# Linear attention and a gated ffn on one core: norm with tokens on partitions, weight conversion on three engines, and two first layers ahead of their second layers

## The chip, the cores and the metric

The kernel runs on one core of a Trainium2 chip. The metric is the device time of one execution in microseconds (us), the median of several executions on the same chip.

## The reference

The input of the ffn is the output of a linear attention whose result is normalized by its root mean square. Cut to what matters:

```python
# q, k, v: (8 batches, 8 heads, 576 tokens, 64) float32
kv  = np.einsum('bhsd,bhse->bhde', k, v)
out = np.einsum('bhsd,bhde->bhse', q, kv)
rms = np.sqrt(np.mean(out * out, axis=-1, keepdims=True) + 1e-06)
attn_out = (out / rms * g_norm).astype(np.float32)

x = attn_out.transpose(0, 2, 1, 3).reshape(4608, 512)
# w_gate, w_val: (512, 1536), w_out: (1536, 512), all float64
gate = 1.0 / (1.0 + np.exp(-(x @ w_gate)))
val  = x @ w_val
return (gate * val @ w_out).astype(np.float32)
```

The weights are float64, so the kernel gets each value as two 32-bit words, and it makes float32 of them for TensorE. There are 36 blocks of 128 x 512 weights: 12 each of w_gate, w_val and w_out.

## The kernel before

The 4608 tokens are cut into 9 chunks of 512. A chunk has 12 steps of first layer (one for each 128 columns of w_gate and w_val) and 4 steps of second layer. The attention of the next batch is cut into 16 small steps (kv, q, u and x for each of four pairs of heads), and one is put in front of each step of a chunk. A kv step makes k^T v of a pair of heads, a q step transposes q, a u step multiplies the two, and an x step makes the ffn's input of the result. The product of gate and value that a step of first layer leaves for the second is called gv. The attention of batch 0 runs alone at the start.

The conversion of a block is seven instructions on VectorE and an add on GpSimd:

```python
        vec.tensor_scalar(out=xf, in0=hi.bitcast(FP32), scalar1=HI_MAX, scalar2=-HI_MAX, op0=ALU.min, op1=ALU.max)
        vec.tensor_scalar(out=y, in0=x, scalar1=0x7FFFFFFF, scalar2=None, op0=ALU.bitwise_and)
        vec.scalar_tensor_tensor(out=yf, in0=yf, scalar=HI_MIN, in1=xf, op0=ALU.is_ge, op1=ALU.mult)
        # y: sign, exponent and the upper 20 bits of the fraction, as a float32.
        vec.tensor_scalar(out=x, in0=y, scalar1=0x07FFFFFF, scalar2=3, op0=ALU.bitwise_and, op1=ALU.logical_shift_left)
        vec.scalar_tensor_tensor(out=y, in0=y, scalar=0xC0000000, in1=x, op0=ALU.bitwise_and, op1=ALU.bitwise_or)
        # x: the lower 32 bits of the fraction, scaled by the power of two that sign and exponent are.
        vec.tensor_scalar(out=x, in0=y, scalar1=0xFF800000, scalar2=None, op0=ALU.bitwise_and)
        vec.scalar_tensor_tensor(out=xf, in0=lo, scalar=2.0 ** -52, in1=xf, op0=ALU.mult, op1=ALU.mult)
        ...
        nc.gpsimd.tensor_tensor(out=flat, in0=xf, in1=yf, op=ALU.add)
```

The norm has channels on partitions. The sum over a head's 64 channels is therefore a matmul with a matrix of ones, whose result is repeated on all channels, and root and reciprocal run over 128 x 576 values:

```python
        def u_step(m):
            ...
                nc.tensor.matmul(ps[:, i, 0:HS], kvs[m % 3], qT[m][:, HS * i:HS * i + HS], start=True, stop=True)
            nc.scalar.copy(out=uT[m]..., in_=ps[:, :, 0:HS])
            nc.vector.tensor_tensor(out=sq[m], in0=uT[m], in1=uT[m], op=ALU.mult)

        def x_step(m):
            ...
                nc.tensor.matmul(ps[:, i, 0:HS], ones, sq[m][:, HS * i:HS * i + HS], start=True, stop=True)
            nc.scalar.activation(out=rs..., in_=ps[:, :, 0:HS], func=AF.Sqrt, bias=eps, scale=1.0)
            nc.vector.reciprocal(rs, rs)
            ...   # xT = uT * g_col * rs on VectorE
```

The order of the steps converts w_gate and w_val one step ahead of their use in chunk 0, and then all of w_out at once:

```python
    for c in range(NG):
        ahead = attention(c + 1) if c + 1 < B else []
        for i, step in enumerate(ffn(c)):        # 12 steps of first layer, 4 of second
            if ahead:
                ahead.pop(0)()
            while done < min(2 * i + 4, 2 * NFT) or i >= NFT - 1 and done < len(units):
                convert(done)
                done += 1
            step()
```

## Time and profile before

| | before |
|---|---|
| time | 1356.22 us, 1355.11 to 1356.49 in 4 runs |
| span of the profiled execution | 1354.3 us |
| attention of batch 0, before the first conversion | 53.4 us |
| from there to the end of chunk 0's first layer | 134.3 us |
| from there to chunk 1's first matmul | 90.7 us |
| the rest | 1075.9 us |

The profile is read here from the stretches that are not full. In the slices of the page each digit is a tenth of busy time of one fortieth of the span; where TensorE has no idle time, as in the first full chunk of this kernel (busy for 137.65 of 137.65 us at a granted clock of 1.00), nothing is to be had but less work for TensorE. In this kernel its row shows 9 from the eighth slice on, and the whole question is what fills the first seven. In the lines PE is TensorE, PEld its weight loads, DVE VectorE, ACT ScalarE, POOL GpSimd, and SP SyncE; the granted clock is the share of TensorE's full clock that the chip allowed. In the lines of a timeline the columns are start, duration, engine, line, operation, result and operands with their shapes, and in brackets the idle time before and what ended it. The lines themselves stand in the prediction.

### The profile page before, as it was taken

The page shows a single profiled execution, that of the slowest core. Times are in us where ns is not written, and L with a number is a line of the kernel's source. Part 1 is how long each engine was busy: PE and PEld are TensorE (multiplying, and loading weights), DVE is VectorE, ACT ScalarE, POOL GpSimd, SP SyncE. Part 2 cuts the span into 40 slices and gives each one's busy share as a digit, 9 for nine tenths or more (in the row PEclk, how much of TensorE's full clock was granted, in tenths as well). Part 3 has the DMA queues.
Part 4 walks back from the last instruction along what each step waited for, and adds up shares of the span by engine and source line. Part 5 has one row for each costly group of instructions (what it writes and reads, how often), then busy time and mean ns, then how long its engine had stood idle before and what let it go on. Part 6 is the DMA issues. An engine that isn't in the chain of part 4 may idle for free.

```text
span 1354.3 us, 9279 instructions
## 1 busy us (share of the span) xinstructions
PE 1260.2 (93%) x3808; PEld 589.2 (44%) x3808; DVE 456.6 (34%) x623; ACT 169.3 (13%) x239; POOL 72.6 (5%) x78
## 2 busy tenths in 40 slices
PE   4578764999999999999999999999999999999998
PEld 3233321444444444444444444444444444444443
DVE  3899999421322223222321332132212221100100
ACT  1100100111211121112111111111112110000000
POOL 0143333000000000000000000000000000000000
PEclk9699885899999999999999999999999999999999
DMA  9244332011101110211020101110100000000000
GB/s 221 57 125 136 106 109 93 24 52 35 27 24 52 35 27 15 60 30 33 16 60 27 32 19 50 36 27 25 42 1 0 15 16 0 0 23 8 0 1 31
DMA packets 61770, 57.23 MB, mean 42 GB/s; under 512 B 40224, under 2 KB 52512, under 8 KB 61728
## 3 DMA queue, kind: packets, MB, share of 16 engines
q1 hardware_dynamic: 51200, 28.32, 8.5%
q0 software_dynamic: 5184, 18.88, 4.4%
q10 hardware_dynamic: 5344, 9.44, 2.0%
q8 instruction: 30, 0.49, 0.2%
q14 instruction: 12, 0.10, 0.0%
HBM read 47.19 MB, written 9.44 MB: 42 GB/s over the span
## 4 chain that ended last, share of the span: by engine, by line
PE 83%; DVE 13%; issue 2%; DMA 1%; ACT 0%; SPq 0%; POOL 0%; POOLq 0%; DVEq 0%; ACTq 0%
PE mm L226 49%; PE mm L235 27%; DVE cy L110 3%; PE at L186 2%; PE at L195 2%; DVE cy L114 2%; DVE cy L111 2%; PE at L165 2%; DVE rs L199 1%; DVE cx L109 1%; DVE cx L113 1%; DVE cx L116 1%; PE at L176 1%; DMA v<-in_v_dram 1%; DVE gv L230 1%
## 5 line engine op out<-in xcount | busy, mean ns | idle before, releaser
L226 PE MATMUL mm<-xT,wg 128*128 128x512 f32 x864 | 399.7, 606 | 27.1 <-POOL wg L120 27.1
L235 PE MATMUL mm<-wo,gv 128*128 128x512 f32 x864 | 389.2, 606 | 32.2 <-POOL wo L120 32.2
L226 PE MATMUL mm<-xT,wv 128*128 128x512 f32 x864 | 389.3, 593 | 8.7 <-POOL wv L120 8.7
L230 DVE TENSOR_TENSOR gv<-mm,sg 128x512 f32<-128x512 f32 x108 | 74.6, 691 | 597.6 <-PE mm L226 597.5
L235 PEld LDWEIGHTS mm<-wo,gv 128*128 128x128 f32 x864 | 165.5, 193 | 240.1 <-issue 188.0
L226 PEld LDWEIGHTS mm<-xT,wv 128*128 128x128 f32 x864 | 163.4, 190 | 218.7 <-issue 202.3
L226 PEld LDWEIGHTS mm<-xT,wg 128*128 128x128 f32 x864 | 161.9, 193 | 204.6 <-issue 170.1
L199 DVE RECIPROCAL rs<-rs 128x576 f32<-128x576 f32 x32 | 120.0, 3752 | 134.4 <-ACT rs L197 134.4
L228 ACT ACTIVATE sg<-mm 128x512 f32<-128x512 f32 x108 | 64.5, 597 | 610.2 <-PE mm L226 610.2
L237 ACT COPY out<-mm 128x512 f32<-128x512 f32 x36 | 21.1, 585 | 397.1 <-PE mm L235 397.1
L190 DVE TENSOR_TENSOR sq<-uT 128x576 f32<-128x576 f32 x32 | 26.0, 811 | 62.4 <-ACT uT L189 62.4
L195 PE MATMUL at<-sq,ones 128*128 128x288 f32 x128 | 38.9, 428 | 5.1 <-DVE sq L190 5.1
L165 PEld LDWEIGHTS at<-v,k 96*64 96x64 f32 x768 | 27.4, 148 | 29.3 <-issue 27.3
L179 DVE COPY qT<-at 128x288 f32<-128x288 f32 x64 | 37.5, 665 | 7.4 <-PE at L176 7.3
L186 PE MATMUL at<-qT,kv 128*128 128x288 f32 x128 | 39.6, 435 | 0.4 <-DVE qT L179 0.4
L165 PE MATMUL at<-v,k 96*64 96x64 f32 x768 | 31.9, 237 | 7.1 <-DMA v<-in_v_dram 6.6
L110 DVE TENSOR_SCALAR cy<-cx 128x512 uint32<-128x512 uint32 x36 | 38.0, 1054 | 1.2
L195 PEld LDWEIGHTS at<-sq,ones 128*128 128x128 f32 x128 | 25.2, 201 | 23.0 <-issue 13.4
L189 ACT COPY uT<-at 128x576 f32<-128x576 f32 x32 | 20.4, 639 | 117.4 <-PE at L186 106.4
L186 PEld LDWEIGHTS at<-qT,kv 128*128 128x128 f32 x128 | 25.9, 205 | 18.9 <-issue 12.7
L176 PEld LDWEIGHTS at<-ident,q 96*128 96x128 f32 x192 | 21.3, 151 | 26.0 <-issue 22.0
L176 PE MATMUL at<-ident,q 96*128 96x96 f32 x192 | 23.2, 261 | 9.9 <-DMA q<-in_q_dram 6.5
(28 smaller groups left out, 305.5 us busy)
## 6 DMA issues: line engine op xcount, KB each, us to landing
k<-in_k_dram SPq DMA_DIRECT2D x32, 288.0 KB, 3.4
v<-in_v_dram SPq DMA_DIRECT2D x32, 288.0 KB, 3.9
q<-in_q_dram SPq DMA_DIRECT2D x64, 144.0 KB, 3.0
out_dram<-out ACTq DMA_DIRECT2D x36, 256.0 KB, 2.0
st<-in_moe_w_gate_dram POOLq DMA_DIRECT2D x12, 512.0 KB, 4.1
st<-in_moe_w_val_dram POOLq DMA_DIRECT2D x12, 512.0 KB, 4.3
st<-in_moe_w_out_dram POOLq DMA_DIRECT2D x12, 512.0 KB, 3.6
g_col<-in_g_norm_dram ACTq DMA_DIRECT2D x2, 0.2 KB, 4.4
```

What stands on the lines that cost most here:

```text
L110: vec.tensor_scalar(out=y, in0=x, scalar1=0x7FFFFFFF, scalar2=None, op0=ALU.bitwise_and)
L111: vec.scalar_tensor_tensor(out=yf, in0=yf, scalar=HI_MIN, in1=xf, op0=ALU.is_ge, op1=ALU.mult)
L165: nc.tensor.matmul(ps[HD * e:HD * e + HD, 0, 0:HD], kin[:, e, js], vin[:, e, js], start=(j == 0), stop=(j == NJ - 1))
L176: nc.tensor.transpose(ps[:, j // 3, c0:c0 + NP], qin[:, j].rearrange("p e d -> p (e d)"), ident[0:NP, 0:NP])
L179: nc.vector.tensor_copy(out=qT[m].rearrange("q (p i t) -> q i t p", i=2, t=3)[:, i], in_=ps[:, i, 0:HS].rearrange("q (t p) -> q t p", t=3))
L186: nc.tensor.matmul(ps[:, i, 0:HS], kvs[m % 3], qT[m][:, HS * i:HS * i + HS], start=True, stop=True)
L195: nc.tensor.matmul(ps[:, i, 0:HS], ones, sq[m][:, HS * i:HS * i + HS], start=True, stop=True)
L199: nc.vector.reciprocal(rs, rs)
L226: nc.tensor.matmul(ps, w[name, f][:, m, :], xT[c][:, m, :], start=(m == 0), stop=(m == NMT - 1))
L228: nc.scalar.activation(out=sg, in_=pg, func=AF.Sigmoid)
L230: nc.vector.tensor_tensor(out=gv[f], in0=pv, in1=sg, op=ALU.mult)
L235: nc.tensor.matmul(ps, gv[f][:, P * t:P * t + P], w["wo", f], start=(f == 0), stop=(f == NFT - 1))
```

## The change

The intent is to shorten the first seven slices in three ways.

1. **Norm.** The u step computes its result with tokens on partitions (six matmuls, with q transposed as the weights). A head's 64 channels then lie side by side in a row, so the mean of squares is one reduce, and the root and the reciprocal are over 96 x 12 values in place of 128 x 576. The x step is six transposes back, and ScalarE copies the result out with the gain as its scale. The tokens stay in the permuted order of the loads, and the stores put the rows back.
2. **Conversion.** The absolute value goes to ScalarE, the limiting to GpSimd, five instructions stay on VectorE, the add stays on GpSimd.
3. **Order.** The first layers of chunks 0 and 1 both precede their second layers, so w_out is converted one block per step of chunk 1's first layer.

The core of the diff:

```diff
+    def limit(u):
+        x = sb.tile([P, UW], U32, tag="cx", name="cx", bufs=1)
+        a = sb.tile([P, UW], FP32, tag="ca", name="ca", bufs=1)
+        nc.gpsimd.tensor_scalar(out=x.bitcast(FP32), in0=hi.bitcast(FP32), scalar1=HI_MAX, scalar2=-HI_MAX,
+                                op0=ALU.min, op1=ALU.max)
+        nc.scalar.activation(out=a, in_=hi.bitcast(FP32), func=AF.Abs)
+        ranged[u] = x, a
...
-        vec.tensor_scalar(out=xf, in0=hi.bitcast(FP32), scalar1=HI_MAX, scalar2=-HI_MAX, op0=ALU.min, op1=ALU.max)
-        vec.tensor_scalar(out=y, in0=x, scalar1=0x7FFFFFFF, scalar2=None, op0=ALU.bitwise_and)
-        vec.scalar_tensor_tensor(out=yf, in0=yf, scalar=HI_MIN, in1=xf, op0=ALU.is_ge, op1=ALU.mult)
+        vec.scalar_tensor_tensor(out=yf, in0=a, scalar=HI_MIN, in1=xf, op0=ALU.is_ge, op1=ALU.mult)
...      (four more instructions on VectorE as before, with a buffer z of their own)
+        limit(u + 1)
...
         def u_step(m):
+            for j in range(NJ):
+                nc.tensor.matmul(ps[0:NP, j // JH, c0:c0 + P], qT[m][:, j // JH, NP * (j % JH):NP * (j % JH) + NP],
+                                 kvs[m % 2], start=True, stop=True)
+            nc.scalar.activation(out=sq, in_=u, func=AF.Square)
+            nc.vector.tensor_reduce(out=ms..., in_=sq..., axis=AX.X, op=ALU.add)
+            nc.scalar.activation(out=ms, in_=ms, func=AF.Sqrt, bias=eps[0:NP], scale=1.0 / HD)
+            nc.vector.reciprocal(ms, ms)
+            nc.vector.tensor_tensor(out=xn[m]..., in0=u..., in1=ms.unsqueeze(3).to_broadcast(...), op=ALU.mult)
         def x_step(m):
+            for j in range(NJ):
+                nc.tensor.transpose(ps[:, j // JH, c0:c0 + NP], xn[m][...], ident[0:NP, 0:NP])
+                nc.scalar.activation(out=chunk(c)[:, m, o:o + n], in_=ps[:, i, r:r + n], func=AF.Copy, scale=g_col)
...
+    todo = [(0, s) for s in ffn_in(0)] + [(1, s) for s in ffn_in(1)] + [(1, s) for s in ffn_out(0) + ffn_out(1)]
+    for c in range(2, NG):
+        todo += [(c, s) for s in ffn_in(c) + ffn_out(c)]
+    for i, (c, step) in enumerate(todo):
+        if c != last:
+            for a in ahead:      # what is left of the attention of the batch before
+                a()
+            ahead = attention(fed) if fed < B and fed <= c + 1 else []
...
+        while done < min(2 * i + 4, 2 * NFT) or i >= NFT and done < min(NFT + i + 2, len(units)):
```

The change also copies q transposed on ScalarE instead of VectorE, loads two pairs of heads ahead instead of three, puts a pair's x step before the next pair's u step, and issues the stores of the result on SyncE's queue instead of ScalarE's.

More of the change, by code (lines that the diff above doesn't have):

```diff
@@ L14 @@
 ALU = mybir.AluOpType
+AX = mybir.AxisListType
 HI_MIN = struct.unpack("<f", struct.pack("<I", 0x38100000))[0]
@@ L42 @@
     NP = S // NJ
-    HS = S // 2
     NMT = DM // P
@@ L47 @@
     NG = T // G
-    NLD = 3
+    NLD = 2
     NST = 3
@@ L72, in load_pair @@
         pairs[n].append(t)
-    for n in range(NLD):
-        load_pair(n)
     units = []
@@ L85 @@
     assert UW == DM
-    staged, w = {}, {}
+    staged, ranged, w = {}, {}, {}
     def load_unit(u):
@@ L93, in load_unit, with words @@
         nc.gpsimd.dma_start(out=staged[u], in_=src)
+    def words(u):
+        t = staged[u]
+        if len(units[u][3]) == 3:
+            t = t.rearrange("p m f -> p (m f)")
+        t = t.bitcast(U32).rearrange("p (n two) -> p n two", two=2)
+        return t[:, :, 0], t[:, :, 1]
+    def limit(u):
+        if u >= len(units):
+            return
+        lo, hi = words(u)
+        x = sb.tile([P, UW], U32, tag="cx", name="cx", bufs=1)
[4 more added lines that the diff above has]
+        ranged[u] = x, a
@@ L95, in convert @@
     def convert(u):
         name, f, src, shape = units[u]
-        if len(shape) == 3:
-            words = staged[u].rearrange("p m f -> p (m f)").bitcast(U32)
-        else:
-            words = staged[u].bitcast(U32)
-        words = words.rearrange("p (n two) -> p n two", two=2)
-        lo, hi = words[:, :, 0], words[:, :, 1]
-        x = sb.tile([P, UW], U32, tag="cx", name="cx")
+        lo, hi = words(u)
+        x, a = ranged.pop(u)
         y = sb.tile([P, UW], U32, tag="cy", name="cy")
-        xf, yf = x.bitcast(FP32), y.bitcast(FP32)
+        z = sb.tile([P, UW], U32, tag="cz", name="cz")
@@ L106, in convert @@
+        xf, yf, zf = x.bitcast(FP32), y.bitcast(FP32), z.bitcast(FP32)
         vec = nc.vector
-        vec.tensor_scalar(out=xf, in0=hi.bitcast(FP32), scalar1=HI_MAX, scalar2=-HI_MAX, op0=ALU.min, op1=ALU.max)
-        vec.tensor_scalar(out=y, in0=x, scalar1=0x7FFFFFFF, scalar2=None, op0=ALU.bitwise_and)
-        vec.scalar_tensor_tensor(out=yf, in0=yf, scalar=HI_MIN, in1=xf, op0=ALU.is_ge, op1=ALU.mult)
-        vec.tensor_scalar(out=x, in0=y, scalar1=0x07FFFFFF, scalar2=3, op0=ALU.bitwise_and, op1=ALU.logical_shift_left)
@@ L114, in convert @@
-        vec.scalar_tensor_tensor(out=y, in0=y, scalar=0xC0000000, in1=x, op0=ALU.bitwise_and, op1=ALU.bitwise_or)
-        vec.tensor_scalar(out=x, in0=y, scalar1=0xFF800000, scalar2=None, op0=ALU.bitwise_and)
-        vec.scalar_tensor_tensor(out=xf, in0=lo, scalar=2.0 ** -52, in1=xf, op0=ALU.mult, op1=ALU.mult)
+        vec.scalar_tensor_tensor(out=yf, in0=a, scalar=HI_MIN, in1=xf, op0=ALU.is_ge, op1=ALU.mult)
+        vec.tensor_scalar(out=z, in0=y, scalar1=0x07FFFFFF, scalar2=3, op0=ALU.bitwise_and, op1=ALU.logical_shift_left)
@@ L118, in convert @@
+        vec.scalar_tensor_tensor(out=y, in0=y, scalar=0xC0000000, in1=z, op0=ALU.bitwise_and, op1=ALU.bitwise_or)
+        vec.tensor_scalar(out=z, in0=y, scalar1=0xFF800000, scalar2=None, op0=ALU.bitwise_and)
+        vec.scalar_tensor_tensor(out=zf, in0=lo, scalar=2.0 ** -52, in1=zf, op0=ALU.mult, op1=ALU.mult)
+        limit(u + 1)
         t = const.tile(shape, FP32, name=f"{name}{f}")
         flat = t.rearrange("p m f -> p (m f)") if len(shape) == 3 else t
-        nc.gpsimd.tensor_tensor(out=flat, in0=xf, in1=yf, op=ALU.add)
+        nc.gpsimd.tensor_tensor(out=flat, in0=zf, in1=yf, op=ALU.add)
@@ L121, in convert @@
         w[name, f] = t
         load_unit(u + NST)
+    load_pair(0)
     for u in range(NST):
         load_unit(u)
+    for n in range(1, NLD):
+        load_pair(n)
     ident = const.tile([P, P], FP32, name="ident")
-    ones = const.tile([P, P], FP32, name="ones")
     eps = const.tile([P, 1], FP32, name="eps")
     g_col = const.tile([P, 1], FP32, name="g_col")
-    kvs = [const.tile([P, P], FP32, name=f"kv{i}") for i in range(3)]
+    kvs = [const.tile([P, P], FP32, name=f"kv{i}") for i in range(2)]
@@ L137 @@
     nc.vector.memset(eps, 1e-6)
-    nc.vector.memset(ones, 0.0)
-    for e in range(2):
-        nc.vector.memset(ones[HD * e:HD * e + HD, HD * e:HD * e + HD], 1.0 / HD)
     for kv in kvs:
@@ L153, in at_ps @@
         return psum.tile([P, 2, 512], FP32, tag="at", name="at")
+    JH = NJ // 2
     def attention(b):
-        qT, uT, sq = {}, {}, {}
+        qT, xn = {}, {}
         def kv_step(m):
             kin, vin, _ = pairs[NHP * b + m]
-            kv = kvs[m % 3]
+            kv = kvs[m % 2]
             ps = at_ps()
@@ L174, in q_step @@
             for j in range(NJ):
-                c0 = NP * (j % 3)
-                nc.tensor.transpose(ps[:, j // 3, c0:c0 + NP], qin[:, j].rearrange("p e d -> p (e d)"), ident[0:NP, 0:NP])
-            qT[m] = sb.tile([P, S], FP32, tag="qT", name="qT")
-            for i in range(2):
-                nc.vector.tensor_copy(out=qT[m].rearrange("q (p i t) -> q i t p", i=2, t=3)[:, i],
-                                      in_=ps[:, i, 0:HS].rearrange("q (t p) -> q t p", t=3))
+                c0 = NP * (j % JH)
+                nc.tensor.transpose(ps[:, j // JH, c0:c0 + NP], qin[:, j].rearrange("p e d -> p (e d)"), ident[0:NP, 0:NP])
+            qT[m] = sb.tile([P, 2, JH * NP], FP32, tag="qT", name="qT")
+            nc.scalar.copy(out=qT[m], in_=ps[:, :, 0:JH * NP])
             load_pair(NHP * b + m + NLD)
@@ L184, in u_step @@
             ps = at_ps()
-            for i in range(2):
-                nc.tensor.matmul(ps[:, i, 0:HS], kvs[m % 3], qT[m][:, HS * i:HS * i + HS], start=True, stop=True)
-            uT[m] = sb.tile([P, S], FP32, tag="uT", name="uT")
-            sq[m] = sb.tile([P, S], FP32, tag="sq", name="sq")
-            nc.scalar.copy(out=uT[m].rearrange("q (i s) -> q i s", i=2), in_=ps[:, :, 0:HS])
-            nc.vector.tensor_tensor(out=sq[m], in0=uT[m], in1=uT[m], op=ALU.mult)
+            for j in range(NJ):
+                c0 = P * (j % JH)
+                nc.tensor.matmul(ps[0:NP, j // JH, c0:c0 + P], qT[m][:, j // JH, NP * (j % JH):NP * (j % JH) + NP],
+                                 kvs[m % 2], start=True, stop=True)
+            u = ps[0:NP, :, 0:JH * P]
+            sq = sb.tile([NP, 2, JH * P], FP32, tag="sq", name="sq", bufs=1)
+            ms = sb.tile([NP, 2, 2 * JH], FP32, tag="ms", name="ms")
+            xn[m] = sb.tile([NP, 2, JH * P], FP32, tag="xn", name="xn", bufs=1)
+            nc.scalar.activation(out=sq, in_=u, func=AF.Square)
+            nc.vector.tensor_reduce(out=ms.rearrange("p i n -> p (i n)"),
+                                    in_=sq.rearrange("p i (n d) -> p (i n) d", d=HD), axis=AX.X, op=ALU.add)
+            nc.scalar.activation(out=ms, in_=ms, func=AF.Sqrt, bias=eps[0:NP], scale=1.0 / HD)
+            nc.vector.reciprocal(ms, ms)
+            nc.vector.tensor_tensor(out=xn[m].rearrange("p i (n d) -> p i n d", d=HD),
+                                    in0=u.rearrange("p i (n d) -> p i n d", d=HD),
+                                    in1=ms.unsqueeze(3).to_broadcast([NP, 2, 2 * JH, HD]), op=ALU.mult)
         def x_step(m):
             ps = at_ps()
-            for i in range(2):
-                nc.tensor.matmul(ps[:, i, 0:HS], ones, sq[m][:, HS * i:HS * i + HS], start=True, stop=True)
-            rs = sb.tile([P, S], FP32, tag="rs", name="rs", bufs=1)
-            nc.scalar.activation(out=rs.rearrange("q (i s) -> q i s", i=2), in_=ps[:, :, 0:HS],
-                                 func=AF.Sqrt, bias=eps, scale=1.0)
-            nc.vector.reciprocal(rs, rs)
+            for j in range(NJ):
+                c0 = NP * (j % JH)
+                nc.tensor.transpose(ps[:, j // JH, c0:c0 + NP], xn[m][:, j // JH, P * (j % JH):P * (j % JH) + P],
+                                    ident[0:NP, 0:NP])
             s0 = 0
@@ L202, in x_step @@
                 c, o = divmod(S * b + s0, G)
-                n = min(G - o, S - s0)
-                nc.vector.scalar_tensor_tensor(out=chunk(c)[:, m, o:o + n], in0=uT[m][:, s0:s0 + n], scalar=g_col,
-                                               in1=rs[:, s0:s0 + n], op0=ALU.mult, op1=ALU.mult)
+                i, r = divmod(s0, S // 2)
+                n = min(G - o, S // 2 - r)
+                nc.scalar.activation(out=chunk(c)[:, m, o:o + n], in_=ps[:, i, r:r + n], func=AF.Copy, scale=g_col)
                 s0 += n
@@ L209, in attention @@
         for t in range(NHP + 2):
-            for step, m in ((kv_step, t), (u_step, t - 1), (q_step, t), (x_step, t - 2)):
+            for step, m in ((kv_step, t), (x_step, t - 2), (q_step, t), (u_step, t - 1)):
                 if 0 <= m < NHP:
@@ L213, in attention @@
         return steps
+    gv = {}
     def mm_ps():
         return psum.tile([P, 512], FP32, tag="mm", name="mm", bufs=4)
-    def ffn(c):
-        gv = {}
-        def in_step(f):
-            pg, pv = mm_ps(), mm_ps()
-            for ps, name in ((pg, "wg"), (pv, "wv")):
-                for m in range(NMT):
-                    nc.tensor.matmul(ps, w[name, f][:, m, :], xT[c][:, m, :], start=(m == 0), stop=(m == NMT - 1))
-            sg = sb.tile([P, G], FP32, tag="sg", name="sg")
-            nc.scalar.activation(out=sg, in_=pg, func=AF.Sigmoid)
-            gv[f] = sb.tile([P, G], FP32, tag="gv", name="gv", bufs=NFT + 1)
-            nc.vector.tensor_tensor(out=gv[f], in0=pv, in1=sg, op=ALU.mult)
-        def out_step(t):
-            ps = mm_ps()
-            for f in range(NFT):
-                nc.tensor.matmul(ps, gv[f][:, P * t:P * t + P], w["wo", f], start=(f == 0), stop=(f == NFT - 1))
-            ot = sb.tile([P, DM], FP32, tag="out", name="out")
-            nc.scalar.copy(out=ot, in_=ps)
-            nc.scalar.dma_start(out=out[G * c + P * t:G * c + P * t + P, :], in_=ot)
-        return [lambda f=f: in_step(f) for f in range(NFT)] + [lambda t=t: out_step(t) for t in range(G // P)]
@@ new lines, in in_step @@
+    def in_step(c, f):
+        pg, pv = mm_ps(), mm_ps()
+        for ps, name in ((pg, "wg"), (pv, "wv")):
+            for m in range(NMT):
+                nc.tensor.matmul(ps, w[name, f][:, m, :], xT[c][:, m, :], start=(m == 0), stop=(m == NMT - 1))
+        sg = sb.tile([P, G], FP32, tag="sg", name="sg")
+        nc.scalar.activation(out=sg, in_=pg, func=AF.Sigmoid)
+        gv[c, f] = sb.tile([P, G], FP32, tag="gv", name="gv", bufs=2 * NFT)
+        nc.vector.tensor_tensor(out=gv[c, f], in0=pv, in1=sg, op=ALU.mult)
@@ new lines, in store, with out_step @@
+    def store(c, t, ot):
+        r0 = 0
+        while r0 < P:
+            b, s = divmod(G * c + P * t + r0, S)
+            j, p = divmod(s, NP)
+            n = min(P - r0, NP - p)
+            dst = out[S * b:S * b + S, :].rearrange("(p j) d -> j p d", j=NJ)[j, p:p + n, :]
+            nc.sync.dma_start(out=dst, in_=ot[r0:r0 + n])
+            r0 += n
+    def out_step(c, t):
+        ps = mm_ps()
+        for f in range(NFT):
+            nc.tensor.matmul(ps, gv[c, f][:, P * t:P * t + P], w["wo", f], start=(f == 0), stop=(f == NFT - 1))
+        ot = sb.tile([P, DM], FP32, tag="out", name="out")
+        nc.scalar.copy(out=ot, in_=ps)
+        store(c, t, ot)
@@ L242, with ffn_in, ffn_out @@
+    def ffn_in(c):
+        return [lambda f=f: in_step(c, f) for f in range(NFT)]
+    def ffn_out(c):
+        return [lambda t=t: out_step(c, t) for t in range(G // P)]
+    limit(0)
     for step in attention(0):
@@ L246 @@
     done = 2
-    for c in range(NG):
-        ahead = attention(c + 1) if c + 1 < B else []
-        for i, step in enumerate(ffn(c)):
-            if ahead:
-                ahead.pop(0)()
-            while done < min(2 * i + 4, 2 * NFT) or i >= NFT - 1 and done < len(units):
-                convert(done)
-                done += 1
-            step()
-        assert not ahead
+    ahead = []
+    fed = 1
+    todo = [(0, s) for s in ffn_in(0)] + [(1, s) for s in ffn_in(1)] + [(1, s) for s in ffn_out(0) + ffn_out(1)]
+    for c in range(2, NG):
+        todo += [(c, s) for s in ffn_in(c) + ffn_out(c)]
+    last = -1
+    for i, (c, step) in enumerate(todo):
[3 more added lines that the diff above has]
+            ahead = attention(fed) if fed < B and fed <= c + 1 else []
+            fed += bool(ahead)
+            last = c
+        if ahead:
+            ahead.pop(0)()
+        while done < min(2 * i + 4, 2 * NFT) or i >= NFT and done < min(NFT + i + 2, len(units)):
+            convert(done)
+            done += 1
+        step()
+    assert fed == B and not ahead
 _INS = ['q', 'k', 'v', 'g_norm', 'moe_w_gate', 'moe_w_val', 'moe_w_out']
```

## The prediction

> **What bounds the kernel now.** I read the page's first two parts, then the busy time of each engine by stretch, then the timeline of VectorE and GpSimd inside the stretches that are not full.
>
> The page says that TensorE is the bound on average, and the slices say where it is not: the first eight of forty.
>
> ```profile
> PE 1260.2 (93%) x3808; PEld 589.2 (44%) x3808; DVE 456.6 (34%) x623; ACT 169.3 (13%) x239; POOL 72.6 (5%) x78
> ...
> PE   4578764999999999999999999999999999999998
> ...
> DVE  3899999421322223222321332132212221100100
> ```
>
> The stretches were cut at events of the timeline: 53.37 us is the first instruction of the weight conversion, 187.70 the end of the first layer of chunk 0, 278.39 the first matmul of chunk 1. The fourth row is one whole chunk with a batch of attention in it, the last a whole chunk without. Columns: length, busy us and instructions of each engine, granted clock, DMA share, GB/s.
>
> ```profile
> 0.00:53.37 53.37, 24.58 (x176) 18.31 (x176) 28.76 (x40) 9.27 (x11) 3.11 (x9) 0.87 0.69 157
> 53.37:187.70 134.33, 104.05 (x308) 45.98 (x308) 128.82 (x211) 14.41 (x20) 49.96 (x50) 0.92 0.38 116
> 187.70:278.39 90.69, 59.36 (x133) 23.31 (x133) 64.94 (x87) 4.46 (x7) 19.50 (x21) 0.70 0.19 61
> 278.39:416.04 137.65, 137.65 (x441) 65.50 (x441) 36.27 (x44) 20.15 (x28) 0.00 (x0) 1.00 0.12 34
> 1103.42:1227.02 123.60, 123.60 (x289) 54.72 (x289) 8.29 (x12) 10.79 (x17) 0.00 (x0) 1.00 0.02 9
> ```
>
> From 278.39 us on TensorE never stops: a chunk is 288 matmul instructions at 123.60/288 = 0.429 us (82.4 us of first layer, 41.2 of second), and a batch of attention costs it 137.65 - 123.60 = 14.05 us. Before that, 53.37 us is a chain of attention for batch 0, in the next 134 us VectorE is 96% busy (conversion is the bound), and in the next 91 us TensorE waits for the converted w_out. The waits of that third stretch (who waited for whom: us, times, longest) say so:
>
> ```profile
> PEld mm L235 <- POOL wo L120: 49.2, 12, 4.5
> ...
> PE mm L235 <- POOL wo L120: 32.2, 12, 3.7
> ```
>
> One conversion of a block, from the timeline of VectorE and GpSimd (start, duration):
>
> ```profile
> 205.73 1.36 POOL L120 TENSOR_TENSOR wo<-cx,cy 128x512 f32<-128x512 f32 x1 [2.97 <-DVE cx L117]
> 206.01 1.37 DVE L110 TENSOR_SCALAR cy<-cx 128x512 uint32<-128x512 uint32 x1
> 207.41 0.69 DVE L111 SCALAR_TENSOR_TENSOR cy<-cy,cx 128x512 f32<-128x512 f32 x1
> 208.13 0.43 DVE L113 TENSOR_SCALAR cx<-cy 128x512 uint32<-128x512 uint32 x1
> 208.60 0.69 DVE L114 SCALAR_TENSOR_TENSOR cy<-cy,cx 128x512 uint32<-128x512 uint32 x1
> 209.32 0.43 DVE L116 TENSOR_SCALAR cx<-cy 128x512 uint32<-128x512 uint32 x1
> 209.78 0.69 DVE L117 SCALAR_TENSOR_TENSOR cx<-st,cx 128x512 f32<-128x512 uint32 x1
> 210.39 0.42 DVE L109 TENSOR_SCALAR cx<-st 128x512 f32<-128x512 f32 x1
> 210.57 1.36 POOL L120 TENSOR_TENSOR wo<-cx,cy 128x512 f32<-128x512 f32 x1 [2.97 <-DVE cx L117]
> ```
>
> The period is 210.57 - 205.73 = 4.84 us. L110 takes 1.37 us where L113, of the same kind, takes 0.43: it stands still for 0.94 us while GpSimd adds. Without that a block is 3.90 us.
>
> [...]the squaring at 93.99 us (two SBUF inputs) took 1.32 us beside a GpSimd add against 0.76 alone. [...]gv takes 691.
>
> **The change, part by part.**
>
> *Second layers after both first layers.* w_out's 12 blocks now convert one per step of chunk 1's first layer. A step is 6.87 us of TensorE plus about 0.9 of attention; VectorE needs about 4.9 for the block and 0.69 for gv. They hide, and chunk 0's second layer later runs at the full rate, 41.2 us.
>
> *Norm with tokens on partitions.* On VectorE a pair of heads now costs a reduce of 768[...], a reciprocal of 12 (3752/576 x 12, under 0.2), a multiply of 768[...] and the kv copies 0.45: 2.5 us. It was 3.75 + 0.81 + 1.33 + 1.03 (xT) + 0.45 = 7.4. In the steady chunks VectorE had time anyway, so this is worth nothing there. On TensorE, differences between step starts in the steady chunk give kv 0.86, q 0.49, u 1.17, x 0.98 us a step. x becomes six transposes like q (0.49). u streams six times 128 columns in place of 576, 1.33 times as much, with more weight loads: estimate 1.5. Net about zero, 14 us a batch stays.
>
> *Attention of batch 0.* The chain per pair was 3.75 (reciprocal) plus about 5. Now: u[...] (2.3 x 1.33, some 2.7),[...] reciprocal 0.2,[...]: 9 us cold, 7 warm, the last ones shorter as no copy-out stands between. From about 18.6 us, when q of pair 1 is through (it waits for the same transfers as now), four pairs end at 43 to 50: I take 47, against 53.37.
>
> *Conversion over three engines.* VectorE loses L109 (0.42) and L110 (0.43): five instructions, 3 x 0.69 + 2 x 0.43 + 0.1 = 3.0 us of its own. ScalarE takes the absolute value (0.6 us, free). GpSimd takes the limiting, one input and 512 elements[...]. [...]3.0 + 0.94 (add)[...] + 0.2 ([...]as L109 grew from 0.42 to 0.63 in such places) = **4.85 us, what it was before**. Two per step, less 0.5 where the add falls beside gv[...], plus gv 0.65: about 9.6. Times 12 steps = 115, plus attention of batch 1 on VectorE (four kv copies, and two u steps[...]), 6 net: 120 us, not the 93 that TensorE would need. Before, the same stage took 128.7 (53.37 to 182.1).
>
> *A new gap.* Chunk 0 now gives batch 1 only 12 of its 16 steps; u2, x2, u3, x3 run back to back before chunk 1, each waiting on its own chain: 1.5 + ([...]table load 1.28[...]) 3.7 + 0.6, then 1.5 + 3.4 + 0.6[...]: 12.4 us, in which TensorE mostly idles.
>
> The sum: 47 + 120 = 167 last block's words ready, add 1.4, the last half step 3.4, the gap 12.4, kv 0.9: chunk 1 starts at 185. What followed chunk 1's start before was 1354.3 - 278.4 = 1075.9; to it comes chunk 0's second layer, 41.2. 185 + 1117 = 1302, and the run's time is 2 us above the profile's span. I take **1302**.
>
> **Rivals.**
> (a) GpSimd's work does not hold VectorE up, because limit and add fall beside gv, copies and the reduce. A block is then 3.1 us, the stage TensorE-bound at about 95, the end 1277. Against: [...]the squaring shows it for two SBUF inputs.
> (b) GpSimd itself or a handshake becomes the bound: x and a have one buffer, so limit of the next block waits for this block's first VectorE instruction, behind the previous add and a DMA issue[...]. If limit takes 1.5 us, a block takes 5.6 and the end is 1320.
> (c) TensorE's small matmuls (u with 96-column weights) cost 2.2 instead of 1.5: 4 x 0.7 x 6 batches = 17 us on the full path: 1319.
> (d) The tables: two loads per u step on ScalarE, 2.6 us; in full chunks a step of 7 us hides it.
>
> **Range and chances.** The certain part is the 48 us of the third stretch (90.7 against 41.2 and the attention in it), less the 12 gap, plus 6 from the prologue and 9 from conversion. (a) and a warm prologue give 1272; (b) or (c) 1320 to 1326. Slower than 1329 needs two of them. So 1274 to 1326, faster by 2% at 0.92.
>
> **What would show it.** First conversion instruction on VectorE at 43 to 50 us; a block of w_gate at 4.5 to 5.1 us with VectorE instructions stretched by 0.5 to 1 us beside GpSimd's; the two-step period near 9.6; an idle of TensorE around 170 to 185 of about 8 us; w_out blocks never waited for; period of later chunks 137 to 139. It is wrong if the stage of the first layer is TensorE-bound (waits for wg and wv vanish), if GpSimd's limit is over 1.2 us, or if a full chunk grows past 140.

What the sums came to:

- A pair of heads on VectorE came to 2.5 us.
- The chain of a pair in the attention of batch 0 came to 9 us "cold" and 7 "warm". The end at 47 us is the estimate. "Cold" and "warm" stand for slow and fast steps of TensorE: in the kernel before a kv step took 1.55 us at 5.67 us and 0.92 at 27.45.
- A block came to 4.85 us. The sum books all of GpSimd's work in this stream as time lost by VectorE. That was an assumption, from two instructions of the kernel before: L110 at 1.37 us for 0.43, and the squaring at 1.32 us for 0.76. By the trace L110 was 1.37 or 1.38 us in 23 of its 36, each beside an add, while gv kept its 0.69 us beside the add of 93.44 us.
- The two u steps in the stage came to 2.9 us each. The chains in the gap came to 3.7 and 3.4 us and the gap to 12.4.

The 0.6 us of the absolute value and the 1.28 of a table load are near what the trace of the kernel before shows for a sigmoid of 512 elements (597 ns) and for a table load (1283 ns).

## The result, and the profile after

The time is **1301.92 us** (1300.39 to 1302.67 in 4 runs) against 1356.22. The ratio is 0.9601, with a 95% interval of 0.9587 to 0.9614. Here and below a ratio is the mean time of one kernel's fast runs over that of the other's of the same rounds, so it is not quite the ratio of the medians. The profiled execution had a span of 1298.5 us.

The page of the kernel after, busy time and slices:

```profile
PE 1242.4 (96%) x4128; PEld 599.2 (46%) x4128; DVE 292.8 (23%) x451; ACT 254.2 (20%) x417; POOL 108.1 (8%) x114
...
PE   4688879999999999999999999999999999999998
...
DVE  1699955520001110111011101110111001000100
```

TensorE is full from the seventh slice on instead of the eighth, and VectorE's row of nines is three slices long instead of five.

The busy time by stretch, with the columns of the prediction's table. The cuts are at first conversion instruction on VectorE, end of chunk 0's first layer, first matmul of chunk 1, about the end of chunk 1's first layer; the last row is a stretch of full chunks. In the kernel before, the second cut (187.70) lies at the first matmul of the second layer, some 2 us after the last one of the first: an x step of 1.13 us and a wait of 0.94 us stand between.

```profile
0.00:49.41 49.41, 23.03 (x186) 20.62 (x186) 10.39 (x24) 13.26 (x24) 3.79 (x10) 0.77 0.59 140
49.41:167.53 118.12, 100.58 (x355) 46.46 (x356) 109.21 (x146) 36.01 (x58) 74.49 (x72) 0.97 0.45 137
167.53:182.04 14.51, 6.91 (x62) 6.08 (x60) 4.95 (x7) 5.59 (x11) 0.00 (x0) 0.82 0.00 1
182.04:278.00 95.96, 95.96 (x344) 46.90 (x343) 55.44 (x87) 30.06 (x45) 29.78 (x32) 0.99 0.30 87
319.00:457.00 138.00, 138.00 (x464) 65.56 (x463) 15.50 (x28) 25.77 (x39) 0.00 (x0) 1.00 0.14 36
```

The second row is the bound that is left: VectorE is busy for 109 of 118 us, TensorE for 101. The third row is the gap that the prediction expected, with TensorE busy for 6.9 of 14.5 us. In the fourth row w_out is converted (29.8 us on GpSimd) and TensorE never stops.

The spans differ by 55.8 us. Of these, 4.0 come from the attention of batch 0 (53.4 to 49.4), 16.2 from the conversion stage (134.3 to 118.1; some 2 of them are that x step and wait), and 35.6 from everything after chunk 0's first layer (1166.6 to 1131.0). Of that last term 35.0 is the stretch that waited for w_out, 90.7 us, less its second layer of 41.2, which now comes later, and less the new gap of 14.5. The other 0.6 is what follows chunk 1's first matmul, 1075.9 against 1116.5 less 41.2. Six later batches at 13.64 us instead of 14.05 would make 2.5 there; where the other 1.9 went is not traced.

Three groups of the page after (busy us, mean ns, idle before and its cause). No second layer waits for w_out any more, and the two new instructions of the conversion have their durations:

```profile
L264 PE MATMUL mm<-wo,gv 128*128 128x512 f32 x864 | 375.4, 592 | 0.0
...
L108 ACT ACTIVATE ca<-st 128x512 f32<-128x512 f32 x36 | 24.5, 680 | 94.6 <-DVE cy L120 46.3
L106 POOL TENSOR_SCALAR cx<-st 128x512 f32<-128x512 f32 x36 | 32.6, 906 | 95.6 <-DVE cy L120 88.7
```

Now two blocks of the conversion stage on VectorE's timeline, one step of first layer, from gv to gv:

```profile
114.57 0.69 DVE L248 TENSOR_TENSOR gv<-mm,sg 128x512 f32<-128x512 f32 x1
115.17 1.26 DVE L120 SCALAR_TENSOR_TENSOR cy<-ca,cx 128x512 f32<-128x512 f32 x1
...
116.93 1.03 DVE L123 SCALAR_TENSOR_TENSOR cy<-cy,cz 128x512 uint32<-128x512 uint32 x1
...
119.79 1.38 DVE L122 TENSOR_SCALAR cz<-cy 128x512 uint32<-128x512 uint32 x1
121.20 1.10 DVE L123 SCALAR_TENSOR_TENSOR cy<-cy,cz 128x512 uint32<-128x512 uint32 x1
122.33 0.76 DVE L125 TENSOR_SCALAR cz<-cy 128x512 uint32<-128x512 uint32 x1
...
123.73 0.68 DVE L248 TENSOR_TENSOR gv<-mm,sg 128x512 f32<-128x512 f32 x1
```

And GpSimd's timeline beside it:

```profile
115.83 0.79 POOL L90 DMA_DIRECT2D st<-in_moe_w_gate_dram  x1
116.65 0.77 POOL L106 TENSOR_SCALAR cx<-st 128x512 f32<-128x512 f32 x1
119.23 1.65 POOL L130 TENSOR_TENSOR wg<-cz,cy 128x512 f32<-128x512 f32 x1 [1.82 <-DVE cz L126]
120.83 0.79 POOL L90 DMA_DIRECT2D st<-in_moe_w_val_dram  x1
121.66 1.14 POOL L106 TENSOR_SCALAR cx<-st 128x512 f32<-128x512 f32 x1
```

The pair takes 123.73 - 114.57 = 9.16 us. The instructions that are longer than their kind (0.69 for two inputs, 0.43 for a TENSOR_SCALAR) lie beside GpSimd's. L122 at 119.79 takes 1.38, that is 0.95 more, beside the add of 119.23. L123 at 116.93 takes 1.03, that is 0.34 more, beside the limit of 116.65; L123 at 121.20 is stretched in the same way, and in this block L125 at 122.33 loses another 0.33 at the end of its limit. Most pairs of this stage look like this one, but not all: where the limit came later, as at 126.25 us, only one instruction of the block was longer. L120 at 115.17 takes 1.26, that is 0.57 more, beside the rest of the add of 114.62; gv, beside the first part of that add, took its usual 0.69.

The gap between the chunks, on TensorE's timeline:

```profile
167.53 1.47 PE L197 MATMUL at<-kv,qT 128*96 128x128 f32 x12
172.92 0.69 PE L216 MATMUL at<-ident,xn 96*128 96x96 f32 x6 [3.92 <-DVE xn L208]
173.44 2.73 PE L197 MATMUL at<-kv,qT 128*96 128x128 f32 x12
179.85 0.78 PE L216 MATMUL at<-ident,xn 96*128 96x96 f32 x6 [3.68 <-DVE xn L208]
180.56 1.55 PE L176 MATMUL at<-v,k 96*64 96x64 f32 x24
182.04 1.22 PE L244 MATMUL mm<-xT,wg 128*128 128x512 f32 x1
```

These are the four steps of batch 1 that found no place in chunk 0: u, x, u, x, each x waiting for the norm of its u. The idle times of 3.9 and 3.7 us were predicted as 3.7 and 3.4. The second u step took 2.73 us instead of 1.47: the granted clock was 0.51 during it and 1.00 during the first (0.82 over the whole gap).

### The profile page after: what moved, and what is told of

It is laid out like the page before. It is cut to its first block, busy times and chain, and to the rows that moved or that the text cites. A ratio compares the mean times of both kernels' runs of the same rounds, so it can differ in the third digit from the quotient of the medians.

```text
span 1298.5 us, 10116 instructions
## 1 busy us (share of the span) xinstructions
PE 1242.4 (96%) x4128; PEld 599.2 (46%) x4128; DVE 292.8 (23%) x451; ACT 254.2 (20%) x417; POOL 108.1 (8%) x114
## 4 chain that ended last, share of the span: by engine, by line
PE 88%; DVE 8%; issue 1%; DMA 1%; ACT 1%; SPq 0%; POOL 0%; DVEq 0%; ACTq 0%
PE mm L244 52%; PE mm L264 29%; PE at L197 3%; DVE cy L123 2%; PE at L176 2%; DVE cz L122 2%; DVE cy L120 2%; PE at L216 1%; DVE cz L125 1%; PE at L187 1%; DMA v<-in_v_dram 1%; DVE xn L208 1%; DVE gv L248 1%; DVE ms L204 0%; DMA q<-in_q_dram 0%
## 5 line engine op out<-in xcount | busy, mean ns | idle before, releaser
L244 PE MATMUL mm<-xT,wg 128*128 128x512 f32 x864 | 395.5, 601 | 11.4 <-POOL wg L130 11.4
L204 DVE TENSOR_REDUCE ms<-sq 96x12 f32<-96x768 f32 x32 | 30.3, 948 | 168.6 <-ACT sq L203 168.6
L197 PEld LDWEIGHTS at<-kv,qT 128*96 128x96 f32 x384 | 50.5, 180 | 14.6 <-issue 13.6
L197 PE MATMUL at<-kv,qT 128*96 128x128 f32 x384 | 53.2, 294 | 0.3 <-ACT xT L224 0.3
L203 ACT ACTIVATE sq<-at 96x768 f32<-96x768 f32 x32 | 25.8, 807 | 94.0 <-PE at L197 94.0
L224 ACT ACTIVATE xT<-at,g_col 128x288 f32<-128x288 f32 (+8 forms) x96 | 33.5, 421 | 54.5 <-PE at L216 54.5
L216 PE MATMUL at<-ident,xn 96*128 96x96 f32 x192 | 23.3, 261 | 20.7 <-DVE xn L208 20.7
L108 ACT ACTIVATE ca<-st 128x512 f32<-128x512 f32 x36 | 24.5, 680 | 94.6 <-DVE cy L120 46.3
L106 POOL TENSOR_SCALAR cx<-st 128x512 f32<-128x512 f32 x36 | 32.6, 906 | 95.6 <-DVE cy L120 88.7
L123 DVE SCALAR_TENSOR_TENSOR cy<-cy,cz 128x512 uint32<-128x512 uint32 x36 | 37.1, 1031 | 1.2
L189 ACT COPY qT<-at 128x576 f32<-128x576 f32 x32 | 20.4, 638 | 86.4 <-PE at L187 86.4
```

What stands on the lines that cost most here:

```text
L106: nc.gpsimd.tensor_scalar(out=x.bitcast(FP32), in0=hi.bitcast(FP32), scalar1=HI_MAX, scalar2=-HI_MAX, op0=ALU.min, op1=ALU.max)
L197: nc.tensor.matmul(ps[0:NP, j // JH, c0:c0 + P], qT[m][:, j // JH, NP * (j % JH):NP * (j % JH) + NP], kvs[m % 2], start=True, stop=True)
L204: nc.vector.tensor_reduce(out=ms.rearrange("p i n -> p (i n)"), in_=sq.rearrange("p i (n d) -> p (i n) d", d=HD), axis=AX.X, op=ALU.add)
L216: nc.tensor.transpose(ps[:, j // JH, c0:c0 + NP], xn[m][:, j // JH, P * (j % JH):P * (j % JH) + P], ident[0:NP, 0:NP])
L224: nc.scalar.activation(out=chunk(c)[:, m, o:o + n], in_=ps[:, i, r:r + n], func=AF.Copy, scale=g_col)
L244: nc.tensor.matmul(ps, w[name, f][:, m, :], xT[c][:, m, :], start=(m == 0), stop=(m == NMT - 1))
```

## The experiments

The theory after this reading was that VectorE's conversion stream is still the bound up to chunk 1, that GpSimd's instructions in it hold VectorE up (0.95 us at an add and 0.34 at a limit in the blocks above), and that the order is worth the waits for w_out less the gap. The first four runs take the parts apart. "Before" in each group is the kernel before, run on the same chip. Where an expectation says "theory", it is this one.

### The order alone undone

```diff
-    todo = [(0, s) for s in ffn_in(0)] + [(1, s) for s in ffn_in(1)] + [(1, s) for s in ffn_out(0) + ffn_out(1)]
...
+    for c in range(NG):
+        ahead = attention(c + 1) if c + 1 < B else []
+        for i, step in enumerate(ffn_in(c) + ffn_out(c)):
...
+            while done < min(2 * i + 4, 2 * NFT) or i >= NFT - 1 and done < len(units):
```

> The changed kernel with one part undone: each chunk does its first layer and then its second, as before. Theory: the 12 blocks of w_out are converted again while TensorE waits for them, 12 x 4.65 us in place of the first of four second-layer steps, so chunk 0's second layer takes about 90 us and not 45: +45; the 14.5 us gap before chunk 1 goes, as chunk 0 has 16 steps again: -14. About 1333 us (1325 to 1340). Rival, that the order is worth what it looks like without the gap: 1347.

It took 1332.80 us (1332.57 to 1333.32) against 1355.44, a ratio of 0.9833 (0.9819 to 0.9848). The waits of this kernel in the stretch where w_out is converted (who waited for whom: us, times, longest) are those of the kernel before again:

```profile
PEld mm L264 <- POOL wo L130: 44.9, 12, 4.4
...
PE mm L264 <- POOL wo L130: 28.2, 11, 3.6
```

From the first matmul of the second layer to chunk 1's first the stretch took 87.2 us, against 90.5 before. The time lies in the expected range. The order of the layers is worth 1332.8 - 1301.9 = 30.9 us on top of the other two parts.

### The old conversion in the kernel after, and the new one in the kernel before

In the first run the seven instructions of VectorE come back, with their two buffers; norm and order stay new. In the second the kernel before gets the new conversion and nothing else.

> The changed kernel with the conversion of before (seven instructions on VectorE, only the add on GpSimd). Theory[...]: a pair of blocks with gv takes 9.87 us as in the kernel before, against 9.24 in the changed one, so 12 x 0.63 = 8 us more: about 1310 (1305 to 1315). Rival, that VectorE's own work counts and GpSimd's is beside it: 0.9 us for each of 24 blocks, 21 us more: 1323.

> The kernel before with the new conversion alone. Theory[...]: 12 x 0.63 us in the first layer of chunk 0 and 12 x 0.2 us for w_out, about 10 us less: 1346 (1340 to 1350). Rival, VectorE's own work: 36 x 0.9 = 32 us less: 1324.

The old conversion took 1314.29 us (1312.41 to 1315.94), ratio 0.9696 (0.9679 to 0.9712). The new conversion alone took 1341.08 us (1340.96 to 1342.31), ratio 0.9896 (0.9881 to 0.9911). So the new conversion is worth 12.4 us in one surrounding and 14.4 in the other, where the prediction's 4.85 us per block, "what it was before", made it worth nothing. In the run with the old conversion a pair of blocks without attention in it took 10.11 to 10.24 us, from gv to gv, against 9.08 to 9.21 in the kernel after. Both runs lie in their expected ranges, near the edge, and some 9 us and more from the rivals. (The 9.87 us for the old pair in the expectation was misread: a kv copy stood in that pair. Beside part of an add kv copies were not longer: two took their usual 0.45 us at 83.64 us in the kernel before, beside the add of 83.22.)

By their order, then: before 1355.4, with the conversion 1341.1, with the norm as well 1332.8, with the order as well 1301.9. Steps of 14.4, 8.3 and 30.9 us; another order of the parts may split them otherwise. The step of the norm holds the small changes too. By the traces of its two ends it is 2.4 us in the attention of batch 0 (the conversion starts at 49.71 us and not 52.09), 3.4 in the conversion stage (113.0 us and not 116.3), and what is left is near the 2.5 us of the six later batches.

### No leftover steps

Batch 1's sixteen steps are spread over the twelve steps of chunk 0, some two at a time, so that none is left for the gap.

```diff
+    TAKE = (2, 2, 1, 2, 1, 1, 2, 1, 1, 1, 1, 1)
...
-        if ahead:
-            ahead.pop(0)()
+        for _ in range(TAKE[i] if i < NFT else 1):
+            if ahead:
+                ahead.pop(0)()
```

> The changed kernel, but batch 1's 16 steps of attention are spread over the 12 first-layer steps of chunk 0 (two in some), so that none is left before chunk 1. Theory: the gap of 14.5 us goes, while two more u steps of 2.5 us each fall on VectorE in the stage that it bounds: 8 to 10 us less, about 1293 (1289 to 1297). Rival, that the gap only moves to another wait: 1302.

It took 1290.51 us (1289.53 to 1292.49), ratio 0.9523 (0.9509 to 0.9537), inside the expected range. Chunk 1 started at 172.81 us instead of 182.04. So 9.2 us of the 14.5 us gap was loss that another order avoids; the rest is work that now lies in the conversion stage. The span of the gap was predicted; that it need not be there is the first gain that the change left.

### Which of the three engines brought the conversion's gain?

The change moves two instructions from VectorE. The next runs put the limiting back on VectorE, do the limiting on GpSimd twice, and put both limiting and add on VectorE, so that GpSimd does nothing but issue loads. The absolute value stays on ScalarE in all three.

```diff
-        nc.gpsimd.tensor_scalar(out=x.bitcast(FP32), in0=hi.bitcast(FP32), scalar1=HI_MAX, scalar2=-HI_MAX,
-                                op0=ALU.min, op1=ALU.max)
...
+        vec.tensor_scalar(out=xf, in0=hi.bitcast(FP32), scalar1=HI_MAX, scalar2=-HI_MAX, op0=ALU.min, op1=ALU.max)
...      (the third run also)
-        nc.gpsimd.tensor_tensor(out=flat, in0=zf, in1=yf, op=ALU.add)
+        vec.tensor_tensor(out=flat, in0=zf, in1=yf, op=ALU.add)
```

> The changed kernel with the limiting moved from GpSimd back to VectorE (0.42 us there), the absolute value still on ScalarE. Theory[...]: VectorE gains 0.45 us of work per block and loses the stalls of about 0.34 us beside the limiting, which in every other block come twice: between 1297 and 1307, no clear change. Rival, that the limiting on GpSimd is free: 24 x 0.45 = 11 us more, 1313.

> The changed kernel with the limiting done twice on GpSimd (the same result written twice; VectorE's work is the same). Theory[...]: each added instruction stops VectorE for another 0.34 us or so in each of 24 blocks: 8 us more, about 1310 (1306 to 1318). Rival, GpSimd's work is beside VectorE's and its own queue (about 3.4 us of a 4.6 us period) has room: 1302.

> The changed kernel with limiting and add both on VectorE; GpSimd only issues the loads of the weights. VectorE's own work per block grows from 3.0 to 3.0 + 0.45 + 0.72 = 4.17 us. Theory[...]: that is what a block takes in the changed kernel on average ((9.24 - 0.6) / 2 = 4.32), so no loss: 1296 to 1303. Rival, GpSimd takes work off VectorE: 24 x 1.17 = 28 us more, 1330.

| kernel | median us | range | ratio to before | pair of blocks, us |
|---|---|---|---|---|
| after | 1301.92 | 1300.39 to 1302.67 | 0.9601 | 9.16 |
| limit on VectorE | 1301.44 | 1300.13 to 1301.91 | 0.9597 | 9.07 |
| limit and add on VectorE | 1301.63 | 1301.27 to 1302.67 | 0.9604 | 9.01 |
| limit twice on GpSimd | 1310.15 | 1308.70 to 1311.14 | 0.9666 | 9.75 |
| old conversion (from above) | 1314.29 | 1312.41 to 1315.94 | 0.9696 | 10.11 to 10.24 |

All three new runs lie in their expected ranges. (The kernel before took 1355.4 us beside them and 1356.2 beside the kernel after; the ratios take that out.) While VectorE bounds the stage, the limiting is worth nothing on GpSimd, and even the add, which the kernel before already had there, is worth nothing: 1301.6 with GpSimd idle. A second limit costs 8.2 us. Its timeline shows an L125 and an L127 of the usual kinds at 1.03 and 0.75 us, in place of 0.69 and 0.43:

```profile
121.60 1.03 DVE L125 SCALAR_TENSOR_TENSOR cy<-cy,cz 128x512 uint32<-128x512 uint32 x1
122.67 0.75 DVE L127 TENSOR_SCALAR cz<-cy 128x512 uint32<-128x512 uint32 x1
```

The kernel with the old conversion and the one with the limit on VectorE differ in the absolute value alone (and one more buffer for the temporaries): 1314.3 against 1301.4. So the whole gain of the new conversion, 12.9 us, is ScalarE's absolute value. The instruction itself, with the gap after it, is 0.46 us in each of 24 blocks, 11 us. The rest is, by the traces, a stretch that it had on VectorE: in the old conversion it took 0.62 us in place of 0.43 in most first blocks of a pair. In the kernel before it shows as follows, beside nothing but the issue of a load (the add had ended at 115.84 us):

```profile
115.79 0.77 POOL L93 DMA_DIRECT2D st<-in_moe_w_gate_dram  x1
116.16 0.62 DVE L110 TENSOR_SCALAR cy<-cx 128x512 uint32<-128x512 uint32 x1
```

Of the three engines of the new conversion only ScalarE brought anything in this order of the steps.

### Loads issued by SyncE

In the kernel after, one block of the pair held a second stall of 0.33 us beside the same limit. There the issue of a load (0.79 us at 120.83) stands before the limit (121.66), and L123 has begun by then (121.20). In the run with GpSimd idle the issue stretched nothing, but there it lay beside two-input instructions (0.69 us) and one early TENSOR_SCALAR (0.42 us); the L110 shown above was longer beside an issue alone. This run moves the issue to SyncE.

```diff
-        nc.gpsimd.dma_start(out=staged[u], in_=src)
+        nc.sync.dma_start(out=staged[u], in_=src)
```

> The changed kernel with the loads of the weights issued by SyncE's queue and not by GpSimd, which then only limits and adds. In the changed kernel every other block shows two VectorE instructions stretched by 0.34 us where GpSimd issued a load and limited. Theory, that one of the two comes with the load's issue on GpSimd: it goes, and a pair of blocks takes 8.9 us and not 9.2, 12 x 0.34 = 4 us in all: about 1298. Rival, that both come from the limiting: the pair stays at 9.2. The loads also change places in the queue at the start, so the pair's period is what decides, not the total (1292 to 1306).

It took 1296.30 us (1295.38 to 1297.17) against 1356.14, ratio 0.9560 (0.9547 to 0.9573). On VectorE's timeline the second stall is gone:

```profile
119.00 0.68 DVE L248 TENSOR_TENSOR gv<-mm,sg 128x512 f32<-128x512 f32 x1
...
126.83 0.43 DVE L125 TENSOR_SCALAR cz<-cy 128x512 uint32<-128x512 uint32 x1
...
127.89 0.68 DVE L248 TENSOR_TENSOR gv<-mm,sg 128x512 f32<-128x512 f32 x1
```

This pair takes 8.89 us (others without attention 8.76 or 8.77), and L125 its 0.43. The conversion stage takes 109.0 us instead of 113.2, and it starts at 47.46 us instead of 49.41. Together that is 6.2 us, of which the gap before chunk 1 takes 0.9 back (15.4 us instead of 14.5; its two x steps took 1.19 us each in place of 0.69 and 0.78). So the second stall goes with the issue. What it is made of stays open: without the issue the limit also starts earlier, at 125.39 us, ahead of the L123 of 125.75, as it does in the other block of the pair above (116.65, ahead of 116.93), which had only one stall with an issue in front of its limit. So it may be the issue itself or where the limit comes to stand, and no run parts the two. The issue can hold an instruction by itself: L110 in the kernel before lost 0.19 us, and so did its like in the run with the old conversion (0.62 us at 124.10 us). Beside a two-input instruction and with nothing else on GpSimd it showed no such stretch (0.69 us at 116.92 us in the run with the limit on VectorE).

### A better order of the conversion

With the stage bound by VectorE from 49 us on, and VectorE only 21% busy before that (10.39 of 49.41 us), the next step was to convert six blocks inside the attention of batch 0, together with the spread of the attention's steps from above.

```diff
-    for step in attention(0):
+    for n, step in enumerate(attention(0)):
         step()
-    convert(0)
-    convert(1)
+        if n in (1, 3, 5, 9, 12):
+            convert(done)
+            done += 1
+    convert(done)
...
-        while done < min(2 * i + 4, 2 * NFT) or ...
+        while done < min(2 * i + 8, 2 * NFT) or ...
```

> The changed kernel with batch 1's steps spread as in e4, and the first six blocks of weights converted inside the attention of batch 0, where VectorE is 21% busy. Theory: the first layer of chunk 0 becomes bound by TensorE, about 94 us in place of 113, and the gap goes; the attention of batch 0 gets 2 to 5 us longer: about 1275 (1268 to 1284). Rival, that the loads of the weights or the waits in VectorE's queue stretch the attention of batch 0 by what is won: 1290 and more.

It took 1280.35 us (1280.26 to 1280.50), ratio 0.9446 (0.9432 to 0.9460): inside the range expected, 5 us above its middle. On TensorE's timeline one of its waits:

```profile
137.13 1.20 PE L216 MATMUL at<-ident,xn 96*128 96x96 f32 x6 [5.78 <-DVE xn L208]
```

An x step waited 5.78 us for VectorE's norm. With two blocks converted per step while TensorE's step was shorter than VectorE's, the reduce of the norm stood behind conversions in VectorE's queue (it ran at 134.39 us). The next run's expectation speaks of 9 us; the wait was 5.78. So the next run keeps the same six blocks ahead and spreads the other 18 evenly over eleven steps.

```diff
-        while done < min(2 * i + 8, 2 * NFT) or ...
+        while done < min(6 + -(-18 * (i + 1) // 11), 2 * NFT) or ...
```

> As e9, but the conversions in chunk 0 are spread evenly over its steps (18 blocks over 11 steps) and not run as far ahead as possible. In e9 TensorE stood still for 9 us before the transposes of the third pair of heads, whose multiply on VectorE was queued behind conversions. Theory, that this order in VectorE's queue is what kept e9 from its expected 1275: 1270 to 1276. Rival, that VectorE has no time left in this stage whatever the order (18 x 4.3 + 12 x 0.6 + 12 of attention = 97 us, against TensorE's 94): 1278 to 1282.

It took 1268.68 us (1268.29 to 1269.69) against 1356.14, ratio 0.9358 (0.9345 to 0.9371), 1.3 us below the range expected. The conversion stage of this kernel, by stretch:

```profile
56.00:160.00 104.00, 104.00 (x402) 51.61 (x401) 92.62 (x131) 42.23 (x66) 56.77 (x59) 0.99 0.46 136
```

TensorE is busy for all of it, and VectorE has pauses. Whether GpSimd's part is still worth nothing when VectorE has pauses is a question of its own, and the last two runs ask it: the even conversion with limit and add on VectorE, and the even conversion with the loads on SyncE.

> As e10, with limiting and add on VectorE as in e7, so that GpSimd only issues loads. Theory[...]: as e10 within 3 us. Rival, that where VectorE has pauses (in the attention of batch 0 and where it waits for TensorE) GpSimd's work does run beside it: 24 x 1.17 us at most, in part, so 5 us or more above e10.

> e10 with the loads of the weights on SyncE's queue. e10 is bound by TensorE in chunk 0's first layer, so a shorter block is worth nothing there: as e10, 1266 to 1270. Rival, that the later landing of the second pair of heads (the weights now precede it in one queue) lengthens the attention of batch 0: 1272 or more.

With GpSimd idle it took 1272.73 us (1272.06 to 1273.50), ratio 0.9387 (0.9375 to 0.9400), which is 4.1 us more than with GpSimd's part, with intervals that do not touch. That is outside the 3 us of the theory and short of the rival's 5 or more. Chunk 0's first matmul came 2.1 us later (55.99 and not 53.86), and two x steps in the stage waited for VectorE's norm, 1.4 us together, where none did with GpSimd's part. So where VectorE has pauses, part of GpSimd's work does run beside it. With the loads on SyncE it took 1266.94 us (1266.33 to 1269.76), ratio 0.9347 (0.9334 to 0.9361), not clearly different from 1268.68, as expected. This is the fastest of the twelve: 6.5% under the kernel before and about 2.7% under the kernel after.

## Why the prediction was right, and where its steps were off

The time was predicted as 1302 us and measured as 1301.9, but that agreement is closer than the steps deserve. They are, in order:

| step | predicted us | measured us |
|---|---|---|
| attention of batch 0, to the first conversion | 47 | 49.4 |
| conversion stage | 120 | 113.2 |
| last add, last half step | 1.4 + 3.4 | 1.4 + 3.5 |
| gap, and kv of chunk 1 | 12.4 + 0.9 | 14.5 |
| from chunk 1 to the end | 1117.1 | 1116.5 |
| span | 1302 | 1298.5 |

The conversion stage is counted to the last VectorE instruction of its 24th block. The span came out 3.7 us lower than the sum. The time lies some 2 us above the span, which the prediction said and then did not add, and the profiled execution was 1.5 us faster than the median. So an error of -6.8 us was covered by +2.4, +1.2 and by the missing 2: the stages are right to a few us each, and the agreement to 0.1 us is luck.

**Order of the layers: right.** No second layer waits for w_out (idle 0.0), the second layer runs at its full rate (592 ns a matmul), and undoing the order alone brought the wait and 30.9 us back. The third stretch less the gap, 48 - 12, was the prediction's "certain part"; it measured 35.0.

**Norm: right.** VectorE's pair of heads takes 0.95 for the reduce, 0.22 for the reciprocal, 0.95 for the multiply and 0.44 for the kv copies: 2.57 us against 2.5 predicted. In the full chunks it was to be worth about nothing; a batch costs TensorE 13.64 us instead of 14.05, since the u step takes 1.31 us and not the 1.5 of the estimate. Rival (c), small matmuls of 2.2 us, is out. Rival (d), the table loads: there are 45 of them, of 1283 ns each, fewer than two for each of the 32 u steps, and in a full chunk TensorE waits for none (busy for 138.00 of 138.00 us). The attention of batch 0 got shorter by 4.0 us, not 6.

**Gap: right in place and kind**, 14.5 us against 13.3. What was missing is the lower clock that was granted there (0.82 over the gap): one u step of 2.73 us at 0.51 and a kv step of 1.55 at 0.50. The prediction also took the gap as given; the run without leftover steps shows that most of it was avoidable.

**Conversion: the step that failed.** It is the sum of 3.0, 0.94 for the add, a term for the limit and 0.2 for a load's issue: "4.85 us, what it was before". The kind of the argument held: VectorE stays the bound (busy for 109 of 118 us), it loses time beside limit and add (0.34 and 0.95 us), and rival (a), GpSimd's work for free, is out (118 us, not 95). The sizes of its terms did not hold. A limit is 0.65 us long when it runs alone (at 8.90 us), but holds VectorE for 0.34 us, in one block of a pair for 0.67; a second limit in each block cost the pair 0.59. The 0.2 for an issue was read off L109 of the kernel before, which took 0.63 or 0.64 us in four places: in three an add's tail lay beside it as well, and in one (74.09 us) the issue alone. L110 after it lost 0.19 beside an issue alone in four blocks. The change removes both. Nor was the pair before what the step took it for: with the old conversion it took 10.1 to 10.2 us. So the step holds two errors. "What it was before" should have come to 124.5 us for the stage, which is what the run with the old conversion shows, and not to 120; and the new conversion took 11.3 of these off. In all it was worth 12 to 14 us. The prediction's list of ranges has "9 from conversion", but that is the whole stage, 128.7 less 120; with a block as long as before, all of it would have had to come from the attention's work on VectorE, which gave some 3. The prediction's own terms for a pair, 2 x 4.85 - 0.5 + 0.65, moreover make 9.85 and not the 9.6 that it wrote; the measured 9.16 is two times 3.0, 0.69 of gv, adds of 0.95 and 0.57, and three stalls of 0.34, which make 9.2. Twelve pairs at 0.42 less than 9.6 are 5.0 of the 6.8 us. The other 1.8 are about what the two u steps were overestimated by: a pair with one took 11.04 or 11.06 us, 1.9 more than a pair without, where the prediction had 2.9.

**Rival (b)**, a limit of 1.5 us or a wait for its buffer, did not come. Limit took 0.91 us on average, and the pair was shorter than assumed.

The experiments add what the prediction did not see: moving the limit to GpSimd has no measurable effect while VectorE bounds the stage (1301.4 without it): the 0.43 us that it saves on VectorE come back there in stalls of 0.34 or 0.67. The gain is the absolute value on ScalarE, beside which VectorE loses nothing: in the run with GpSimd idle it still runs, and no instruction of VectorE in the pair from 115.64 us on is longer than its kind (0.69 and 0.43 us).

## What to carry to other kernels

In this kernel, with VectorE the bound and its two-input and TENSOR_SCALAR instructions back to back, an instruction moved to GpSimd gained nothing (1301.4 and 1301.9 us), and one moved to ScalarE gained at least its full length (12.9 us for 24 of 0.43); only where VectorE had pauses was GpSimd's part worth something (4.1 us). In another kernel, look for such stretched instructions before moving work to GpSimd. A stage is not only bound by its sum: work that a later stage of another engine needs goes one piece per step into a stage with slack (the order of the layers was worth 30.9 us here), steps left over at a boundary are a serial chain (spreading sixteen steps over twelve took 11.4 us away), and work that another engine waits for must not queue behind a burst (spreading 18 blocks evenly took 11.7 us away). A prediction that hits the total is checked by its terms all the same: here an error of 7 us was covered by smaller ones of the other sign.
